# Gated recurrence and capacity routing into eight experts: a shorter routing chain ahead of the experts, with both instruction orders fitted again

## The chip, the cores and the metric

The kernel runs on one core of one Trainium2 chip. The metric is device microseconds of one execution, as a median of several runs. One core has TensorE (PE, matmul), VectorE (DVE), ScalarE (ACT), GpSimd (POOL) and SyncE (SP, which issues transfers), each with its own instruction queue, and 16 DMA engines.

## The reference

Two stages, cut to what matters. The first is a recurrence over 768 steps for 4 x 8 heads of width 48; its output becomes 3072 tokens of width 384. The second gives every token to one of 8 experts, with exactly 384 places each, by going through all token-expert scores in falling order.

```python
for t in range(S):                                  # a normalised to at most 0.999 in magnitude
    S_re, S_im = ar * S_re - ai * S_im + kv[t], ar * S_im + ai * S_re
    y[:, :, t] = einsum('bhd,bhde->bhe', q[:, :, t], S_re)
x = y.transpose(0, 2, 1, 3).reshape(N, DM)          # N = 3072, DM = 384
logits = x @ w_gate                                 # [N, 8]
for idx in argsort(-logits.flatten()):              # cap = N // 8
    tok, e = idx // 8, idx % 8
    if assigned[tok] < 0 and counts[e] < cap:
        assigned[tok] = e; counts[e] += 1
for e in range(8):
    out[assigned == e] = relu(x[assigned == e] @ w1[e]) @ w2[e]
```

## The kernel before, in words

**First half** (`attention`). The 3072 tokens go in 24 units of 128, in eight groups of three. VectorE, ScalarE and GpSimd turn the decay into running products and angles; VectorE rotates keys and queries (`f<-kq,CS`); a transfer restacks them per head; TensorE does scores (`sc`), state (`U`) and output (`y`), and last the pick matmuls (`FN`, tile `xp`), which put a unit's 128 tokens in rows beside their 8 logits. ScalarE evicts the token part (`XE`, tile `x`, stored to DRAM as `xd`), and VectorE reduces the logits (`LR`, tile `lg`). `xp` has a single buffer: the next unit's `FN` waits for this unit's `XE` and `LR`. Where TensorE would idle, filler matmuls (`hot`) are put in.

**Routing** (`Router`). Expert by expert, the kernel looks for the one that fills first. `scale` takes the extremes of all logits across partitions, `quantize` turns scores into 24-bit integers. `find` searches the cut value for all experts at once in five levels of 32 thresholds: VectorE compares all tokens with them (`ind`), TensorE counts (`cnt`), VectorE compares the counts with what is needed (`cs`, `f`), and TensorE adds the step to the thresholds (`thr`). It ends with each token's position in the chosen expert (`pi`) and the expert's weight rows (`eidx`). `slots` turns positions into the expert's list of tokens (`idx`): position = 32 x high + low, two compares give one-hot rows (`o`: 12 and 32 wide), and a count matmul of the low one-hot with the high one-hot, multiplied by the token's row and column number (`rh`), gives them. `update` removes the chosen expert from the scores and picks each token's next best: that readies the next search.

**Second half** (`experts`). GpSimd gathers weights (`w1t`, `w2t`) and tokens (`xg`) by indirect transfers. Expert 0 runs in fp32: transposes (`turn`), first layer (`hidden`), second layer (`last`). Experts 1 to 7 run as three products of split halves (`w1h`, `w1l`, `xh`, `xl`, `hh`, `hl`, `w2h`, `w2l`), the splits made by ScalarE and VectorE. 18 warm-up matmuls stand ahead of expert 0. Route e + 1 runs while expert e is computed, on the same engines.

**Order.** Every operation is first put in a list with a cost, its dependences and a priority; `in_order` plays the list against one queue per engine, and the instructions are then issued in that order, which the engines keep. In the first half the priority is the unit's number plus `OFF[kind]`; in the second it is a due time, reckoned back from the end, less `M_OFF[kind]`. With `slack`, VectorE may be given a less urgent step while an urgent one is about to become ready.

All instructions go through one helper, so the profile's line is L130 almost everywhere and rows are told apart by their tiles.

Of the kernel before, what the change touches and what calls it, by code (L numbers as in the profile page):

```python
# [8 lines left out]
F32 = mybir.dt.float32  # L9
# [3 lines left out]
I32 = mybir.dt.int32  # L13
AF = mybir.ActivationFunctionType
# [23 lines left out]
LEAD_R = 8  # L38
GRID = [2.0 ** 19, 2.0 ** 14, 2.0 ** 9, 2.0 ** 4, 1.0]

# [9 lines left out]
def constants(nc, con, z, w_gate):  # L50
# [20 lines left out]
    t("i32f", [128, 32])  # L71
    t("wd", [128, 8])
    t("cidx", [128, NT])
# [7 lines left out]
    t("lg", [128, NT, E])  # L81
# [3 lines left out]
    t("ext", [128, 2, B])  # L85
# [86 lines left out]
def in_order(ops, step, hop, wait, done_, start, slack, late=None):  # L172
# [23 lines left out]
    while len(done) < len(ops):  # L196
        pick = None
        for e, xs in ready.items():
            if xs:
                t = max(free[e], min(o.at for o in xs))  # L200
                o = min((o for o in xs if o.at <= t), key=lambda o: (o.prio, o.at, o.n))
                if slack and e == "dve":
                    h = min((o for o in xs if o.at <= t + 1.0), key=lambda o: (o.prio, o.at, o.n))
                    if h.prio < o.prio - 1500.0:
                        o = min((o for o in xs if o.at <= t and t + o.cost <= h.at + slack),
                                key=lambda o: (o.prio, o.at, o.n), default=h)
                t = max(t, o.at)
                if pick is None or t < pick[0]:
                    pick = t, o
# [25 lines left out]
def attention(nc, real, tc, z, q, k, a_re, a_im, v_tok, xd, later):  # L235
# [222 lines left out]
    def unit(i):  # L458
# [97 lines left out]
        def logits():  # L556
            v.tensor_reduce(z.lg[:, i], mine["xp"][:, :, 96:104].rearrange("p a e -> p e a"), op=OP.add, axis=AX.X)
            if i % 6 == 5:
                r = slice(i - 5, i + 1)
                lg = z.lg[:, r].rearrange("p c e -> p (c e)")  # L560
                v.tensor_reduce(z.ext[:, 0, b:b + 1], lg, op=OP.max, axis=AX.X)
                v.tensor_reduce(z.ext[:, 1, b:b + 1], lg, op=OP.min, axis=AX.X)
# [77 lines left out]
OFF = {"A1": 7.7532, "F1": -8.0, "F10": -0.2852, "F11": 6.1629, "F2": 1.0958, "F3": 3.1048, "F4": 3.0098, "F5": -8.0, "F6": 8.0, "F7": -6.5322, "F8": 3.2365, "F9": 5.0508, "FL": 2.946, "FL<": -3.9259, "FN": 4.3835, "G1": -0.6071, "G2": 4.4992, "G3": 8.0, "G4": -8.0, "G5": -5.9505, "K": 1.9006, "KC": -0.4768, "LR": -3.8173, "MK": -2.5243, "MX": -4.6482, "N0": 0.976, "N1": -8.0, "N2": -5.5169, "P0": -6.2872, "R0": -7.514, "R1": -4.516, "R2": 3.2639, "R3": 4.827, "R4": -4.8476, "R5": -0.5791, "S": 6.954, "SC": 3.4101, "SC<": -8.0, "ST": 0.3675, "ST<": -0.421, "T1": 7.9956, "T2": 6.9667, "T3": -8.0, "TL": 5.7027, "UA": -3.4084, "UA<": -5.1223, "WM": 0.1274, "XC": 7.799, "XC<": -7.3842, "XE": 4.4086, "XS": 0.7846, "la": -5.6357, "later": -8.0, "li": -5.3368, "lk": -1.3428, "lv": 6.2134, "RK": -2.7051, "RQ": -3.6666, "table": -0.5748, "CA": 3.7656, "BE": -7.9653}  # L640
# [6 lines left out]
class Router:  # L647
# [11 lines left out]
    def masks(self, nc):  # L659
# [6 lines left out]
        g.iota(z.i32f, pattern=[[1, 32]], base=0, **kw)  # L666
        g.iota(z.wd, pattern=[[-1, 8]], base=8, **kw)
        g.iota(z.cidx, pattern=[[1, NT]], base=0, **kw)
# [36 lines left out]
    def scale(self):  # L705
        nc, z, v, t, ps = self.nc, self.z, self.nc.vector, self.mine, self.ps
        mm = t("mm", [128, 2])
        low = t("low", [128, B])
        v.tensor_scalar(low, z.ext[:, 1], -1.0, None, op0=OP.mult, op1=OP.max, accum_out=mm[:, 0:1])
        v.tensor_reduce(mm[:, 1:2], z.ext[:, 0], op=OP.max, axis=AX.X)  # L710
        mp = ps.tile([2, 128], F32, name="sm")
        nc.tensor.transpose(mp, mm, z.ident)
        m2 = t("m2", [2, 1])
        v.tensor_reduce(m2, mp, op=OP.max, axis=AX.X)
        gp = ps.tile([128, 2], F32, name="sm")
        nc.tensor.matmul(gp, m2.to_broadcast([2, 128]), z.mask[:2, :2], start=True, stop=True)
        gm = t("gm", [128, 1])
        rg = t("rg", [128, 2])
        v.tensor_scalar(rg[:, 0:1], gp[:, 1:2], 1e-30, 1.0 / KMAX, op0=OP.max, op1=OP.mult)
        v.tensor_copy(gm, gp[:, 0:1])  # L720
        v.reciprocal(rg[:, 1:2], rg[:, 0:1])
        self.gm, self.rg = gm, rg[:, 1:2]
        r = slice(NT - 6, NT)
        best(nc, z, self.wk, z.lg[:, r], z.top[:, r], z.qm[:, r], z.oh[:, r])
        self.m, self.qm, self.oh = t("m0", [128, NT]), z.qm, z.oh
        self.quantize(self.m, z.top)

    def quantize(self, key, x):
        v = self.nc.vector
        ki = self.wk.tile(x.shape, I32, name="ki")  # L730
        v.tensor_scalar(ki, x, self.gm, self.rg, op0=OP.add, op1=OP.mult)
        v.tensor_copy(key, ki)

    def merge(self, out, x, n, less=None):
        v = self.nc.vector
        part = [x[32 * c:32 * c + 32, n * c:n * c + n] for c in range(4)]
        if less is None:
            v.tensor_copy(out, part[0])
# [5 lines left out]
    def keys(self):  # L744
        self.key = self.mine("key", [128, NT, E])
        self.quantize(self.key, self.z.lg)

    def find(self, parts, by_pe, more):
# [17 lines left out]
        w = NT // parts  # L766
        for it in range(len(GRID)):
            ind = t("ind", [128, NT, 32], BF)
            for c in range(0, NT, w):
                v.tensor_tensor(ind[:, c:c + w], bc(m[:, c:c + w], 32),  # L770
                                thr[:, None, 32 * it:32 * it + 32].to_broadcast([128, w, 32]), op=OP.is_ge)
            both = ps.tile([128, 128], F32, name="cnt")
            whole = both[:32, :E]
            for lot in range(0, NT, w):
                with nc.one():
                    for c in range(lot, lot + w) if by_pe else ():
                        nc.tensor.matmul(whole, ind[:, c], oh[:, c], start=(c == 0), stop=(c == NT - 1))
                    for c in range(lot, lot + w, 4) if not by_pe else ():
                        nc.tensor.matmul(both[:, :32], ind[:, c:c + 4].rearrange("p c j -> p (c j)"),
# [10 lines left out]
            else:  # L790
                v.tensor_scalar(f, cnt, 0.0, -1.0, op0=OP.is_ge, op1=OP.max, accum_out=fm)
            nc.tensor.matmul(thr[:, 32 * (it + 1):], self.weight[:, it].to_broadcast([32, 128]), fm.bitcast(BF)[:, 1:2].to_broadcast([32, end - 32 * it - 31]),
                             start=False, stop=(it == len(GRID) - 1), skip_group_check=True)
# [34 lines left out]
        up = t("up", [128, NT])  # L828
        v.tensor_tensor(up, ah, qm, op=OP.mult)
        v.tensor_tensor(home, home, up, op=OP.add)  # L830
        tie0 = t("tie0", [128, NT])
        v.scalar_tensor_tensor(tie0, m, lo, free, op0=OP.is_equal, op1=OP.mult)
        rt = t("rt", [128, 2])
        old = t("old", [128, NT])
        v.tensor_scalar(old, home, em, 0.0, op0=OP.is_equal, op1=OP.add, accum_out=rt[:, 0:1])
        tie = t("tie", [128, NT])
        v.scalar_tensor_tensor(tie, qm, em, tie0, op0=OP.is_equal, op1=OP.mult, accum_out=rt[:, 1:2])
        off = ps.tile([128, 2], F32, name="sm")
        nc.tensor.matmul(off, z.tri, rt.bitcast(BF)[:, 1::2], start=True, stop=True)
# [15 lines left out]
        pi = t("pi", [128, NT], I32)  # L855
        v.scalar_tensor_tensor(pi, pos, -1.0, rank, op0=OP.add, op1=OP.add)
# [3 lines left out]
    def rest(self):  # L860
# [22 lines left out]
        pi = t("pi", [128, NT], I32)  # L883
        v.tensor_scalar(pi, pos, -1.0, None, op0=OP.add)
        self.found = eidx, pi

    def update(self, more):
# [16 lines left out]
        v.tensor_tensor(self.key, self.key, kn[:, None].to_broadcast([128, NT, E]), op=OP.add)  # L904
        m, qm, oh = t("m", [128, NT]), t("qm", [128, NT]), t("oh", [128, NT, E], BF)
        best(nc, z, wk, self.key, m, qm, oh)
        v.scalar_tensor_tensor(need, e2, SHUT, cc, op0=OP.mult, op1=OP.subtract)
# [7 lines left out]
    def slots(self, pi, by_pe):  # L915
# [6 lines left out]
        def be(x):  # L922
            return x[:, None].to_broadcast([128, NT, x.shape[1]])

        p2 = t("p2", [128, 2, NT], I32)
        v.tensor_scalar(p2[:, 0], pi, 5, None, op0=OP.arith_shift_right)
# [482 lines left out]
```

## Time and profile before

| | |
|---|---|
| runs, us | 530.4, 530.79, 543.11; median 530.79 |
| profiled execution, us | 533.11, with a span of 531.3 from first to last instruction |
| busy over the span | TensorE 84%, VectorE 78%, ScalarE 52%, GpSimd 14% |
| mean granted TensorE clock | 0.960 of full speed |

The span is the time from the first instruction to the last in one profiled execution; the 1.8 us beside it are outside of all instructions. A matmul's busy time overlaps the next one's, since they are pipelined, so rates are read from start to start.

### The profile page before, as it was taken

The page shows a single profiled execution, that of the slowest core. Times are in us where ns is not written, and L with a number is a line of the kernel's source. Part 1 is how long each engine was busy: PE and PEld are TensorE (multiplying, and loading weights), DVE is VectorE, ACT ScalarE, POOL GpSimd, SP SyncE. Part 2 cuts the span into 40 slices and gives each one's busy share as a digit, 9 for nine tenths or more (in the row PEclk, how much of TensorE's full clock was granted, in tenths as well). Part 3 has the DMA queues.
Part 4 walks back from the last instruction along what each step waited for, and adds up shares of the span by engine and source line. Part 5 has one row for each costly group of instructions (what it writes and reads, how often), then busy time and mean ns, then how long its engine had stood idle before and what let it go on. Part 6 is the DMA issues. An engine that isn't in the chain of part 4 may idle for free.

```text
span 531.3 us, 9644 instructions
## 1 busy us (share of the span) xinstructions
PE 447.5 (84%) x3621; PEld 394.1 (74%) x3630; DVE 415.9 (78%) x1190; ACT 274.4 (52%) x426; POOL 76.0 (14%) x95
## 2 busy tenths in 40 slices
PE   0008889899889999995589899989979999999993
PEld 0007768697769888993478579878978988999993
DVE  5989879899989999735847789798988997946330
ACT  6997859696949686511012524154341544344420
POOL 3000000000000000000121213241221232440202
PEclk9999999899989999996599999999979999999997
DMA  7865879897969676621342404461250621950101
GB/s 247 248 185 153 236 209 278 214 257 210 251 194 281 176 238 178 171 77 44 121 164 107 191 31 143 170 244 64 94 223 31 231 82 39 394 207 1 46 0 44
DMA packets 48909, 86.03 MB, mean 162 GB/s; under 512 B 5344, under 2 KB 43744, under 8 KB 46816
## 3 DMA queue, kind: packets, MB, share of 16 engines
q1 hardware_dynamic: 39104, 42.56, 27.6%
q0 software_dynamic: 6304, 38.16, 21.0%
q10 hardware_dynamic: 3456, 4.72, 2.6%
q8 instruction: 28, 0.46, 0.3%
q14 instruction: 17, 0.14, 0.1%
HBM read 53.49 MB, written 9.44 MB: 118 GB/s over the span
## 4 chain that ended last, share of the span: by engine, by line
PE 49%; DVE 18%; DMA 13%; ACT 7%; issue 6%; SPq 4%; POOL 1%; another core or an unknown queue 0%; POOLq 0%; ACTq 0%; DVEq 0%
PE acc L130 30%; SPq L130 4%; PE y L130 4%; ACT s L130 4%; PE U L130 3%; DMA s<-s 3%; PE sc L130 3%; DMA ar<-in_a_re 3%; PE xp L130 3%; DVE hl L130 2%; PE cnt L130 2%; DMA V<-in_v 2%; DVE f L130 2%; DMA KQ<-f 2%; DVE p L130 1%
## 5 line engine op out<-in xcount | busy, mean ns | idle before, releaser
L130 PE MATMUL sc<-KQ 96*128 96x128 f32 x384 | 50.2, 284 | 41.3 <-DMA KQ<-f 41.3
L130 PEld LDWEIGHTS sc<-KQ 96*128 96x128 f32 x384 | 47.3, 197 | 44.6 <-DMA KQ<-f 42.1
L130 ACT ACTIVATE hh<-acc 128x384 fp32r<-128x384 f32 x56 | 27.3, 492 | 74.6 <-PE acc L130 69.2
L130 PE MATMUL acc<-w2h,hh 128*128 128x384 f32 x168 | 53.5, 351 | 0.1
L130 PE MATMUL acc<-w2l,hh 128*128 128x384 f32 x168 | 53.4, 352 | 0.1
L130 PE MATMUL acc<-w2h,hl 128*128 128x384 f32 x168 | 53.4, 353 | 0.0
L130 PE MATMUL acc<-xh,w1h 128*128 128x384 f32 x168 | 51.0, 348 | 0.5 <-DVE hl L130 0.5
L130 PE MATMUL acc<-xh,w1l 128*128 128x384 f32 x168 | 50.2, 343 | 0.0
L130 PE MATMUL acc<-xl,w1h 128*128 128x384 f32 x168 | 49.8, 341 | 0.0
L130 DVE TENSOR_TENSOR f<-kq,CS 128x768 f32<-128x768 f32 x48 | 43.5, 951 | 0.2 <-ACT CS L130 0.2
L130 DVE SCALAR_TENSOR_TENSOR hl<-acc,hh 128x384 fp32r<-128x384 f32 x56 | 30.4, 550 | 15.0 <-ACT hh L130 14.5
L130 DVE TENSOR_TENSOR ind<-m,thr 128x768 bf16<-128x768 f32 (+1 forms) x40 | 33.7, 850 | 10.3 <-PE thr L130 9.8
L130 POOL DMA_INDIRECT out<-ot,idx x24 | 25.5, 1062 | 108.6 <-ACT ot L130 98.7
L130 ACT ACTIVATE ot<-acc 128x384 f32<-128x384 f32 x24 | 11.8, 490 | 54.7 <-issue 29.4
L130 PE MATMUL y<-am,V 128*64 128x128 f32 x384 | 37.0, 281 | 1.7 <-ACT xT L130 1.2
L130 DVE TENSOR_TENSOR am<-sc,mask 128x512 f32<-128x512 f32 x48 | 32.1, 683 | 5.0 <-PE sc L130 4.9
L130 PE MATMUL xp<-pick,xT 112*128 112x104 f32 x192 | 27.7, 290 | 8.6 <-ACT xT L130 5.7
L130 PEld LDWEIGHTS xp<-pick,xT 112*128 112x128 f32 x192 | 25.0, 201 | 12.1 <-ACT xT L130 7.3
L130 PEld LDWEIGHTS acc<-xh,w1h 128*128 128x128 f32 x168 | 30.8, 188 | 2.4 <-DVE hl L130 0.9
L130 PEld LDWEIGHTS acc<-w2l,hh 128*128 128x128 f32 x168 | 31.9, 193 | 0.9 <-DVE w2l L130 0.3
L130 PEld LDWEIGHTS acc<-w2h,hh 128*128 128x128 f32 x168 | 31.6, 192 | 0.8 <-DVE hl L130 0.5
L130 PEld LDWEIGHTS acc<-w2h,hl 128*128 128x128 f32 x168 | 31.5, 193 | 0.4
(186 smaller groups left out, 1064.4 us busy)
## 6 DMA issues: line engine op xcount, KB each, us to landing
KQ<-f SPq DMA_DIRECT2D x192, 96.4 KB, 2.4
kq<-in_k SPq DMA_DIRECT2D x8, 576.0 KB, 4.8
kq<-in_q SPq DMA_DIRECT2D x8, 576.0 KB, 6.1
V<-in_v SPq DMA_DIRECT2D x8, 576.0 KB, 9.5
xd<-x ACTq DMA_DIRECT2D x24, 192.0 KB, 2.9
ar<-in_a_re SPq DMA_DIRECT2D x6, 576.0 KB, 4.8
ai<-in_a_im SPq DMA_DIRECT2D x6, 576.0 KB, 5.8
s<-s POOLq DMA_DIRECT2D x6, 576.0 KB
```

Source lines behind the costliest of these rows:

```text
L130: r = f(*a, **k)
```

## The change

1. *Logits then eviction.* The last unit's eviction waits for its logits reduce. Extremes are taken twice, over units 0 to 17 and over the last six with the first result, in place of four times; both get across partitions by two matmuls against the identity and a reduce over 128. Scores are quantized straight into integers, without a cast.
2. *Search levels.* The first search compares in three lots of 8 units in place of two of 12, with the counts of each lot behind it, and the threshold matmul of a level is split: first the 32 columns that the next level reads.
3. *Slots in 16 bits.* Positions, one-hots and token numbers are kept as pairs of 16-bit values, so that the compares and the product have all operands in 16 bits with an innermost row of 2. One token number replaces row and column number, so `rh` is 12 wide and ScalarE's part goes. The 32-wide compare is made in two halves with the count matmuls of each behind it.
4. *Next search deferred.* What belongs to the next search (`need`, `home`) has the priority kind of `update`, the first route's steps may not be held up by slack fillers, and `hidden(0)` comes ahead of `turn(1)` in the list.
5. All values of `OFF` and `M_OFF` are new (of the logits reduce `LR` from -3.8173 to 6.6491, of the eviction `XE` from 4.4086 to -2.5219), as are some costs of the planner (`M_STEP` 0.15 to 0.12, an indirect transfer's issue 1.04 to 1.26).

```diff
-        op(("XE", i), "act", 0.46, at, out, [("FN", i), ("XS", i - 2)])
+        op(("LR", i), "dve", 0.15 if i not in (MOST - 1, NT - 1) else 0.45, at, logits, [("FN", i)])
+        op(("XE", i), "act", 0.46, at, out, [("FN", i), ("XS", i - 2)] + ([("LR", i)] if i == nu - 1 else []))
-        op(("LR", i), "dve", 0.15 if i % 6 < 5 else 0.45, at, logits, [("FN", i)])
...
+        for i in range(2):
+            nc.tensor.matmul(gp[:, i], z.ext[:, i:i + 1].to_broadcast([128, 128]), z.ident, start=True, stop=True)
+        for i, o in enumerate((OP.max, OP.min)):
+            v.tensor_reduce(lim[:, i], gp[:, i], op=o, axis=AX.X)
...
-        v.tensor_scalar(ki, x, self.gm, self.rg, op0=OP.add, op1=OP.mult)
-        v.tensor_copy(key, ki)
+        self.nc.vector.tensor_scalar(key, x, self.gm, self.rg, op0=OP.subtract, op1=OP.mult)
...
+            at = 32 * (it + 1)
+            for lo, hi in ((at, at + 32), (at + 32, end + 1)) if first and at < end else ((at, end + 1),):
+                nc.tensor.matmul(thr[:, lo:hi], self.weight[:, it].to_broadcast([32, 128]), fm.bitcast(BF)[:, 1:2].to_broadcast([32, hi - lo]),
+                                 start=False, stop=(it == len(GRID) - 1), skip_group_check=True)
...
+        if first:
+            v.tensor_tensor(home, ah, qm, op=OP.mult)
+        if more:
+            v.scalar_tensor_tensor(need, e2, SHUT, cc, op0=OP.mult, op1=OP.subtract)
...
-        nc.scalar.activation(rh[:, :, 0], o12, AF.Copy, scale=z.pid)
-        o32 = t("o32", [128, NT, 32], BF)
-        v.tensor_tensor(o32, be(z.i32f), bc(p2[:, 1], 32), op=OP.is_equal)
-        v.tensor_tensor(rh[:, :, 1], o12, bc(z.cidx, 12), op=OP.mult)
+        rh = t("rh", [128, NT, 6, 2], F16)
+        v.tensor_tensor(rh, o12, z.token[:, :, None].to_broadcast([128, NT, 6, 2]), op=OP.mult)
+        o32 = t("o32", [128, 2, NT // 2, 16, 2], F16)
+        for h in range(2):
+            c0 = h * NT // 2
+            v.tensor_tensor(o32[:, h], row(32, NT // 2),
+                            hl[:, 1][:, c0:c0 + NT // 2, None].to_broadcast([128, NT // 2, 16, 2]), op=OP.is_equal)
...
+        hidden(0)
         turn(1)
-        hidden(0)
...
-PARTS = (2, 1, 1, 1, 1, 1, 1)
+PARTS = ((0, 8, 16),) + 6 * ((0,),)
```

## Rows read from the trace of the kernel before

**Rows 1.** Busy time by stretch, us: sum and count per engine, granted clock, DMA share, GB/s.
```profile
60.00:220.00 160.00, 146.51 (x1467) 125.97 (x1473) 148.23 (x273) 121.95 (x160) 3.37 (x4) 0.98 0.80 224
...
390.00:400.00 10.00, 7.34 (x30) 6.24 (x30) 7.38 (x24) 3.44 (x4) 2.85 (x3) 0.66 0.30 95
400.00:520.00 120.00, 119.69 (x754) 112.91 (x753) 83.28 (x264) 48.55 (x102) 29.10 (x28) 1.00 0.30 114
```

**Rows 2.** Instructions in order of time, last logits to first compare: start us, duration us.
```profile
241.88 0.49 ACT L130 ACTIVATE x<-xp 128x384 f32<-128x384 f32 x1 [1.45 <-PE xp L130]
...
242.40 0.19 DVE L130 TENSOR_REDUCE lg<-xp 128x8 f32<-128x32 f32 x1 [1.75 <-ACT x L130]
...
243.38 0.37 PE L130 MATMUL sm<-ident,mm 128*2 128x128 f32 x1 [0.44 <-DVE mm L130]
...
245.84 0.55 DVE L130 TENSOR_TENSOR ind<-m,thr 128x384 bf16<-128x384 f32 x1
```

**Rows 3.** The same view inside the first search.
```profile
249.91 0.23 PE L130 MATMUL thr<-fm,weight 32*128 32x97 bf16 x1 [0.25 <-DVE f L130]
250.19 1.02 DVE L130 TENSOR_TENSOR ind<-m,thr 128x384 bf16<-128x384 f32 x2 [0.25 <-PE thr L130]
...
250.79 0.95 PE L130 MATMUL cnt<-oh,ind 128*32 128x8 bf16 x24 [0.65 <-DVE ind L130]
...
254.05 0.18 PE L130 MATMUL thr<-fm,weight 32*128 32x33 bf16 x1 [0.25 <-DVE f L130]
```

**Rows 4.** The same view, end of the first search to the gather.
```profile
256.27 0.16 DVE L130 COPY ends<-thr 128x2 f32<-128x2 f32 x1 [0.17 <-PE thr L130]
...
258.83 1.05 POOL L130 DMA_INDIRECT w1t<-in_w,eidx  x1 [119.27 <-DVE need L130]
...
261.14 1.31 DVE L130 TENSOR_TENSOR o<-i32f,p 128x288 bf16<-128x288 f32 x2
...
262.75 0.94 DVE L130 TENSOR_TENSOR ind<-m,thr 128x768 bf16<-128x768 f32 x1
...
262.87 0.82 PE L130 MATMUL cnt<-rh,o 128*32 128x24 bf16 x24 [3.00 <-DVE rh L130]
...
264.38 0.66 DVE L130 SCALAR_TENSOR_TENSOR idx<-ic 32x3 int32<-32x3 f32 x4
...
265.31 0.99 POOL L130 DMA_INDIRECT xg<-xd,idx  x1 [5.42 <-DVE cs L130]
```

**Rows 5.** The same view, transposes to the first product of expert 0.
```profile
269.18 0.36 PEld L130 LDWEIGHTS acc<-ident,xg 128*128 128x128 f32 x3
...
271.10 0.49 ACT L130 ACTIVATE x<-acc 128x384 f32<-128x384 f32 x1 [8.90 <-PE thr L130]
...
271.64 1.60 PE L130 MATMUL acc<-x,w1t 128*128 128x128 f32 x12 [1.21 <-ACT x L130]
```

**Rows 6.** VectorE's groups by shape, 241 us to the end: busy us, mean ns.
```profile
L130 DVE TENSOR_TENSOR o<-i32f,p 128x768 bf16<-128x768 f32 x8 | 7.6, 947 | 0.0
...
L130 DVE TENSOR_TENSOR ind<-m,thr 128x384 bf16<-128x384 f32 x10 | 5.2, 549 | 0.9 <-PE thr L130 0.9
...
L130 DVE TENSOR_TENSOR o<-i32f,p 128x288 bf16<-128x288 f32 x8 | 3.6, 448 | 0.0
```

**Rows 7.** Instructions in order of time, TensorE alone, among the experts.
```profile
302.25 0.20 PE L130 MATMUL thr<-fm,weight 32*128 32x97 bf16 x1 [2.20 <-DVE f L130]
...
307.90 0.63 PE L130 MATMUL acc<-xh,w1h 128*128 128x384 f32 x1
308.37 0.81 PE L130 MATMUL acc<-w2t,h 128*128 128x384 f32 x2
...
393.57 0.34 PE L130 MATMUL cnt<-oh,ind 128*128 128x32 bf16 x6 [1.24 <-DVE ind L130]
```

**Rows 8.** TensorE's groups from 308.3 to 313.6 us: busy us, mean ns.
```profile
L130 PE MATMUL acc<-w2t,h 128*128 128x384 f32 x13 | 5.4, 492 | 0.0
```

**Rows 9.** What TensorE waited for: us in total, times, longest us.
```profile
PE xp L130 <- DVE lg L130: 0.8, 1, 0.8
```

More of the change, by code (lines that the diff above doesn't have):

```diff
@@ L13 @@
 I32 = mybir.dt.int32
+I16 = mybir.dt.int16
 AF = mybir.ActivationFunctionType
@@ L37, with twice @@
 SHUT = 8192.0
-LEAD_R = 8
+MID = N // 2
+MOST = NT - 6
+PAIR = 1 + (1 << 16)
 GRID = [2.0 ** 19, 2.0 ** 14, 2.0 ** 9, 2.0 ** 4, 1.0]
+def twice(x):
+    return x[:, :, None].to_broadcast([128, NT, 2])
 def bc(x, n):
@@ L204, in in_order @@
                     if h.prio < o.prio - 1500.0:
-                        o = min((o for o in xs if o.at <= t and t + o.cost <= h.at + slack),
+                        o = min((o for o in xs if o.at <= t and t + o.cost <= h.at + (0.0 if h.kind == "first" else slack)),
                                 key=lambda o: (o.prio, o.at, o.n), default=h)
@@ L737, in merge @@
         if less is None:
-            v.tensor_copy(out, part[0])
+            v.tensor_scalar(out, part[0], more, None, op0=OP.add)
         else:
@@ L933, in slots @@
-        o32 = t("o32", [128, NT, 32], BF)
-        v.tensor_tensor(o32, be(z.i32f), bc(p2[:, 1], 32), op=OP.is_equal)
-        v.tensor_tensor(rh[:, :, 1], o12, bc(z.cidx, 12), op=OP.mult)
+        rh = t("rh", [128, NT, 6, 2], F16)
+        v.tensor_tensor(rh, o12, z.token[:, :, None].to_broadcast([128, NT, 6, 2]), op=OP.mult)
+        o32 = t("o32", [128, 2, NT // 2, 16, 2], F16)
         both = ps.tile([128, 128], F32, name="cnt")
-        with nc.one():
-            for c in range(NT) if by_pe else ():
-                nc.tensor.matmul(both[:32, :24].rearrange("p (a k) -> p a k", a=2), o32[:, c], rh[:, c],
-                                 start=(c == 0), stop=(c == NT - 1))
-            for c in range(0, NT, 4) if not by_pe else ():
-                nc.tensor.matmul(both[:, :96], o32[:, c:c + 4].rearrange("p c j -> p (c j)"),
-                                 rh[:, c:c + 4].rearrange("p c a k -> p (c a k)"), start=(c == 0), stop=(c == NT - 4))
@@ L944, in slots @@
-        ic = t("ic", [32, 2, 12])
+        for h in range(2):
+            c0 = h * NT // 2
+            v.tensor_tensor(o32[:, h], row(32, NT // 2),
+                            hl[:, 1][:, c0:c0 + NT // 2, None].to_broadcast([128, NT // 2, 16, 2]), op=OP.is_equal)
+            w = 1 if by_pe else 4
+            with nc.one():
+                for c in range(0, NT // 2, w):
+                    nc.tensor.matmul(both[:32 * w, :12 * w], o32[:, h][:, c:c + w].rearrange("p c a b -> p (c a b)"),
+                                     rh[:, c0 + c:c0 + c + w].rearrange("p c a b -> p (c a b)"),
+                                     start=(c0 + c == 0), stop=(c0 + c == NT - w))
@@ L945, in slots @@
+        idx = t("idx", [128, 3], I32, bufs=8)
         if by_pe:
[L946 to L953 removed]
+            with nc.one():
+                for s in range(4):
+                    v.tensor_scalar(idx[32 * s:32 * s + 32], both[:32, s:12:4], float(MID), None, op0=OP.add)
+        else:
+            ic = t("ic", [32, 12])
+            self.merge(ic, both, 12, more=float(MID))
+            with nc.one():
+                for s in range(4):
+                    v.tensor_copy(idx[32 * s:32 * s + 32], ic[:, s::4])
@@ L1128, in call @@
                 rate, base = RATE[self.e]
+                if name == "tensor_tensor" and all(mybir.dt.size(x.dt if isinstance(x, View) else x.dtype) == 2 for x in a):
+                    rate *= 2
                 cost = n / rate + base
```

138 lines of the change are left out of this document (62 added, 76 removed).

## The prediction

> **What bounds the kernel now.** I read busy time by stretch of time first [rows 1], then the instructions in order of time through the gap between the two halves [rows 2 to 5], then VectorE's groups by operation [rows 6], and last what TensorE waits for later [rows 7 to 9]. Three regimes follow. From 60 to 220 us VectorE is busy 148.2 of 160 us and TensorE only 146.5 with fillers in it, so the first half goes at VectorE's pace; it has 11.8 us of idle in all for a better order to win. From 400 to 520 TensorE is busy 119.7 of 120 at the full clock: there only fewer matmuls would help [rows 1]. Between them lies the gap that this change is about: the last units' results leave TensorE at 241.88 and the first product of expert 0 starts at 271.64 [rows 2, 5]. In these 29.8 us almost nothing runs but one chain of small steps: scale, five search levels, slots, gather, transposes. A microsecond taken from that chain is a microsecond for expert 0, since nothing else is late there.
>
> **Scale and first quantizing.** Before, the last logits reduce waits for the eviction of the same tile (x from 241.88, lg from 242.40), and the first search compare starts at 245.84 [rows 2]: 3.96 us from the start of x, 3.44 from the start of lg. After, the reduce starts at once: 0.52 saved. What follows it is estimated from VectorE's groups: 768 elements take 0.947 and 288 take 0.448 [rows 6], so 1.04 ns an element on a fixed part of 0.15, and operations that don't depend on each other overlap by some 0.08. After: the reduce 0.19, two extremes over 50 elements 0.32, two fp32 matmuls against the identity (0.37 by [rows 2]; the second bounded by 0.1 and 0.4, I take 0.2), two reduces over 128 elements 0.48, three dependent steps of 0.2 with their hops, a quantize of 0.3 straight to integers, three hops to and from TensorE of 0.1: near 2.75, against 3.44. Sum: 0.52 + 0.69, **-1.2** (bounds -0.5, if the choice of the last six units queues between these steps, and -1.6).
>
> **Five levels.** Two levels take 254.05 - 249.91 = 4.14 us, 2.07 each: threshold matmul 0.23, two compares 1.02 together, 24 count matmuls 0.95 that overlap the second compare, then the verdict [rows 3]. In three lots the compares cost one more fixed part: from 0.95 for 768 and 0.55 for 384 elements [rows 6] a 256-element one is 0.41, and three with the usual overlap of 0.08 make 1.09, +0.07. Behind the last compare lie 8 count matmuls and not 12, 0.04 each by 0.95 / 24: -0.16. The split threshold matmul lets the next compare start after 32 columns; the 33-column one took 0.18 against 0.23 for 97 columns [rows 3]: -0.03 on average, or +0.05 if the compare still waits for both pieces. Sum 0.1 a level, **-0.5** (bounds -0.8 and +0.2).
>
> **From the search to the gather.** Before: ends at 256.27, slot compares at 261.14, gather on POOL at 265.31 [rows 4]. In the first 4.87 us VectorE also runs the next search's six 192-element steps (0.35 each by that slope, 0.27 with the overlap) and seven steps of 8 or 24 elements (the fixed part 0.15 less the overlap, near 0.08 each), 2.2 in all. After, they are deferred. Some of them sit in bubbles where the chain waits for TensorE's prefix matmul, so I take 1.5 (bounds 0.6 and 2.2). From 261.14 to 265.31 = 4.17: two compares and a product 1.7, 24 matmuls 0.82, then the count's copy waits because the next search's compare was put in front of it (262.75, 0.94), copy, four index writes 0.66, 0.27 to POOL [rows 4]. After: in 16 bits, if VectorE takes two elements a step, half the slope between 288 elements (0.448) and 768 (0.947) [rows 6] gives 0.30 for 288 and 0.35 for 384: 0.30 + 0.30 + 0.35 + 0.35 - 3 x 0.08 = 1.06; then 0.05, the second 12 matmuls 0.41, 0.10, four writes 0.66, 0.27: 2.55. That is -1.6; unpacked the same sum is 3.25, -0.9. ScalarE's product of 24 rows leaves the path; it had run beside the second compare, so I give it nothing. Sum **-3.1** (bounds -1.5 and -4.2).
>
> No row of the kernel before is a two-tensor operation with every operand in 16 bits, so the packed price is bounded by the 1x rows and by half their slope. The Trainium skill (Vector Engine (DVE) Microarchitecture Reference, 5.1 Performance modes) says that a two-source operation takes two elements a cycle when all operands are 2 bytes wide and the innermost step is one, also when a row is read again and again, but that one 2-byte element repeated 16 times as a source ran at one a cycle. That speaks for the pair layout here (innermost row of 2), and by it the sum is 2.55; a layout that merely narrowed the types would stay at 3.25. No run shown yet tests it.
>
> **Gather and first product.** POOL's queue holds the weight load (258.83, 1.05) and then the gathers. The first transposes start at 269.18, 3.87 after the gather's issue, and the first product 2.46 after that, though x waits until 271.10 [rows 4, 5]. Three transposes, an eviction of 0.49 and two hops are about 1.3. The order now puts hidden(0) ahead of the second block's transposes, which were what TensorE held in between; I take **-0.9** (bounds 0 and -1.2). The gather now comes 4.8 sooner, the weight load only by about 2 (scale and levels), so 3.7 and not 6.5 lie between them; if the load still fills the queue the gather lands up to 2.8 later than I count. I take 0, as the product needs those weights anyway. The warm-up matmuls move with the slots; if the clock were still at its lower level, expert 0's first twelve products, 1.60 now [rows 5], would take twice that: cost 0, up to +1.6.
>
> Expert 0 therefore starts 1.2 + 0.5 + 3.1 + 0.9 = **5.7 us** sooner, near 266.
>
> **What is given back.** Route 1's search had its first compare at 262.75, ahead of the indices. Now it comes after them and after the deferred steps: indices end near 260.2, plus about 1.5, so 261.7, a gain of only 1.05; its own slots give 0.7. Expert 1's data are then 1.75 sooner, expert 0's work 5.7 sooner: 3.95 apart. Before, expert 1's first product ran at 307.90 [rows 7] while thirteen second-layer matmuls of expert 0 were still to come [rows 8]; a piece of two takes 0.81 [rows 7] and one alone 0.49, so they are 0.32 apart (4.2 us), so most of the difference has work to cover it. I take **+1.1** (bounds 0 and 4).
>
> **Later routes.** Each sheds about 0.7 us of VectorE time in its slots. TensorE is held by VectorE in two places: 2.20 before the threshold matmul at 302.25, and around 393, where it waits 1.24 for a compare [rows 7]; in 390 to 400 it is busy 7.34 at a mean clock of 0.66 [rows 1], that is 2.7 of idle and up to 3.4 lost at the lower level that follows it. Together up to 8.2. Both waits end on VectorE's search steps, which 0.7 less work shortens but does not remove, and the new order moves all of them. I take **-2.4** (bounds -8.2, and +5 for one more hole with its clock drop, sized like that of 390 to 400).
>
> **The first half's order.** Extremes: six 48-element reduces fewer, two longer ones more, about equal. All 24 units keep their matmuls. 93% busy VectorE sets the pace, so a new order is worth 0, within 3 either way (a quarter of its 11.8 idle).
>
> **Sum.** -5.7 + 1.1 - 2.4 = -7.0. The profiled execution took 533.1 for a span of 531.3; the median of the runs is 530.8, 2.3 under it, and the difference applies to it as it is: **523.8 us**. About 2%, 10.6 us, is what a measurement of this kernel tells from no change, so this counts as within it.
>
> **Rivals.** (1) Expert 1 becomes the bound: route 1 gains little, the 3.95 is given back in full and no later hole closes: 530.8 - 5.7 + 4 = 529, or 531 with a worse hole. For it: VectorE, not TensorE, ends the wait at 302.25. Against: the thirteen covering matmuls. Chance 0.20. (2) The holes close as well: -5.7 and most of the 8.2, with the clock staying up: 517, down to 514 with a better first half. For it: the drop around 393 is a consequence of one wait, and one wait less removes all of it. Against: nothing in the change touches a search level of a later route. Chance 0.27. (3) Slower: the logits reduce gets late in the first half. Its due time moves from -3.8 to +6.6, and the pick matmuls of the next unit wait for it, the PSUM tile being single. Before, TensorE waited so once, 0.8 [rows 9]. If in each of 24 units the reduce sits behind one more step of 0.95, that is +22.8: 530.8 - 7 + 22.8 = 546.6. It decides once the reduce falls past the next unit's pick matmuls; units are several microseconds apart except the last three, which speaks against it. Chance 0.07. (4) The 16-bit steps run at one element a cycle, like the rows of today [rows 6]. Slots 0.7 slower in the gap, 5.0 and not 5.7 saved, and of the later holes only a third of the relief: 530.8 - 5.0 + 1.1 - 0.8 = 526.1. For it: in every slot step one operand is still one value read 6 or 16 times over, now as a pair; against: the pair itself fills the 4 bytes that one fp32 value filled. Chance 0.08. (By the rule of the Trainium skill named above this would happen only where the innermost row is one repeated element.) The forecast itself: 0.38.
>
> **Range and chances.** The forecast's own range is 520 to 528. To hold 8 in 10 it takes in (4), most of (1) and most of (2): 514 to 532. Faster by over 2% (under 520.2): 0.27 from (2) and 0.04 from the forecast's low end, 0.31. Slower by over 2% (over 541.4): 0.06 from (3). Within: 0.63.
>
> **What would show it.** In the profile after: the last logits reduce ahead of the last eviction; 2.75 from it to the first compare; levels of about 1.97; 16-bit compares of 0.30 and 0.35; the gather 4 to 5 us and expert 0's first product 5 to 6 us nearer to the end of the first half; indices before any compare of the next search. The prediction falls if the first half's end moves by more than 3 us, if a hole like that at 393 opens or vanishes, or if TensorE stands still between expert 0 and expert 1.

## The result, and the profile after

The changed kernel takes **540.26 us** in the median of 20 runs (534.65 to 556.19); the kernel before, on the same chips, 533.91 (20 runs). The ratio is 1.0106, 95% interval 1.0069 to 1.0144: about 1.1% slower, where 523.8 us and a range of 514 to 532 were predicted. Ratios here and below leave disturbed executions out; medians don't. The profiled execution took 539.48 us, span 537.7.

Busy time by stretch of the kernel after, with the columns of [rows 1]:

```profile
60.00:220.00 160.00, 147.04 (x1420) 129.09 (x1427) 139.76 (x252) 116.27 (x150) 3.52 (x3) 0.93 0.73 210
...
300.00:310.00 10.00, 5.78 (x43) 4.01 (x42) 4.93 (x22) 5.49 (x12) 3.85 (x4) 1.00 0.91 371
310.00:320.00 10.00, 9.99 (x35) 5.30 (x36) 6.38 (x15) 2.94 (x5) 0.42 (x1) 0.83 0.01 2
...
390.00:400.00 10.00, 9.81 (x64) 9.03 (x63) 9.78 (x38) 6.42 (x16) 2.77 (x3) 1.00 0.81 327
400.00:520.00 120.00, 119.01 (x751) 111.31 (x750) 87.57 (x288) 50.67 (x102) 33.63 (x30) 1.00 0.32 120
```

Against [rows 1] the first half lost most: VectorE is busy 8.5 us less in the same 160 us (139.8 for 148.2), and TensorE's mean clock fell from 0.98 to 0.93. The hole of 390 to 400 is gone; a new one stands at 300 to 310, with a lower clock behind it.

Three milestones place the 6.4 us between the two profiled executions. The last results of the first half leave TensorE at 250.99 (before 241.84): **+9.15**. From there to expert 0's first product it is 27.23 (before 29.80): **-2.57**. From the first product to TensorE's end it is 250.9 (before 251.06): **-0.2**.

The gap after, instructions in order of time: start us, duration us, engine; it answers to [rows 2 to 5].

```profile
251.02 0.19 DVE L137 TENSOR_REDUCE logits<-xp 128x8 f32<-128x32 f32 x1 [3.03 <-PE xp L137]
251.25 0.49 ACT L137 ACTIVATE x<-xp 128x384 f32<-128x384 f32 x1 [1.45 <-DVE logits L137]
...
254.29 1.08 DVE L137 TENSOR_TENSOR ind<-m,thr 128x256 bf16<-128x256 int32 x3
...
256.35 1.08 DVE L137 TENSOR_TENSOR ind<-m,thr 128x256 bf16<-128x256 int32 x3 [0.28 <-PE thr L137]
...
264.36 0.16 DVE L137 COPY ends<-thr 128x2 f32<-128x2 f32 x1 [0.17 <-PE thr L137]
...
268.04 0.57 DVE L137 TENSOR_TENSOR o<-k,hl 128x288 f16<-128x288 f16 x2
268.53 0.30 DVE L137 TENSOR_TENSOR rh<-o,token 128x288 f16<-128x288 f16 x1
...
268.75 0.35 DVE L137 TENSOR_TENSOR o<-k,hl 128x384 f16<-128x384 f16 x1
268.88 0.47 PE L137 MATMUL cnt<-rh,o 128*32 128x12 f16 x12 [1.56 <-DVE rh L137]
...
269.28 0.80 PE L137 MATMUL acc<-ident,mask 128*128 128x128 f32 x2
...
269.79 0.95 DVE L137 TENSOR_TENSOR ind<-m,thr 128x768 bf16<-128x768 f32 x1
...
270.01 0.49 PE L137 MATMUL cnt<-rh,o 128*32 128x12 f16 x12
...
271.05 0.36 DVE L137 TENSOR_TENSOR q<-q,wd 128x192 f32<-128x192 f32 x1
271.33 0.64 DVE L137 TENSOR_SCALAR idx<-cnt 32x3 int32<-32x3 f32 x4
...
272.24 0.99 POOL L137 DMA_INDIRECT xg<-xd,idx  x1 [3.69 <-DVE idx L137]
...
276.97 0.49 PE L137 MATMUL acc<-ident,xg 128*128 128x128 f32 x3
...
278.22 1.58 PE L137 MATMUL acc<-x,w1t 128*128 128x128 f32 x12 [0.36 <-ACT x L137]
```

The reader is to see two things. The 16-bit steps are as short as was forecast, 0.30 and 0.35. But the first slot compare at 268.04 and the gather's issue at 272.24 are 4.20 apart, as before (4.17): two warming matmuls (269.28) stand between the halves of the counting matmuls, and the next search's compare (269.79) and two steps on `q` (the last at 271.05) stand in front of the indices (271.33).

In the first half, the two longest pieces of the chain that ended last (start us, length us):

```profile
83.28 10.38 DMA s<-s
...
117.60 9.65 DMA s<-s
```

And three of the waits after (total us, times, longest):

```profile
ACT xT L137 <- PE y L137: 19.6, 11, 4.3
...
ACT s L137 <- DMA s<-s: 10.4, 3, 5.2
...
PE xp L137 <- ACT xT L137: 9.5, 7, 3.3
```

s<-s is an addition that the GpSimd queue does as an accumulating transfer (step F6, for six of the ten blocks). ScalarE then takes the logarithm of the sum (F7), and the eviction xT of TensorE's tokens is queued behind that. ScalarE in order of time:

```profile
90.36 0.49 ACT L137 ACTIVATE x<-xp 128x384 f32<-128x384 f32 x1 [2.86 <-PE xp L137]
93.68 1.25 ACT L137 ACTIVATE s<-s,cb 128x1152 f32<-128x1152 f32 x1 [2.83 <-DMA s<-s]
94.84 1.15 ACT L137 ACTIVATE s<-zi 128x1152 f32<-128x1152 f32 x1
95.89 0.57 ACT L137 ACTIVATE xT<-y 128x512 f32<-128x512 f32 x1
...
106.12 0.60 ACT L137 ACTIVATE xT<-y 128x512 f32<-128x512 f32 x1 [4.35 <-PE y L137]
```

And TensorE at the same time:

```profile
86.75 2.05 PE L137 MATMUL sc<-KQ 96*128 96x128 f32 x16
...
92.39 0.81 PE L137 MATMUL hot<-cold 128*128 128x512 bf16 x3 [0.16 <-issue]
96.52 1.14 PE L137 MATMUL xp<-pick,xT 112*128 112x104 f32 x8 [3.31 <-ACT xT L137]
...
98.16 3.53 PE L137 MATMUL sc<-KQ 96*128 96x128 f32 x16
```

TensorE stands 3.31 us for xT at 96.5; from 98.3 to 108.5 its granted clock is at the lower level, and sixteen products that took 2.05 us at 86.75 take 3.53. ScalarE then waits 4.35 for TensorE. The same happens after 127.3. A third drop begins at 159.7, behind shorter waits of TensorE (0.69 for xT at 155.25, 0.71 and 0.54 for KQ at 157.26 and 158.11). Before, ScalarE waited 2.7 us for these transfers in all.

### The profile page after: what moved, and what is told of

It reads as the page before. It is cut to its first block, busy times and chain, and to the rows that moved or that the text cites. A ratio compares the mean times of both kernels' runs of the same rounds, so it can differ in the third digit from the quotient of the medians.

```text
span 537.7 us, 9586 instructions
## 1 busy us (share of the span) xinstructions
PE 454.4 (84%) x3597; PEld 401.5 (75%) x3607; DVE 410.3 (76%) x1192; ACT 271.8 (51%) x418; POOL 80.1 (15%) x95
## 4 chain that ended last, share of the span: by engine, by line
PE 45%; DMA 15%; DVE 13%; issue 11%; ACT 8%; SPq 4%; POOL 2%; POOLq 0%; DVEq 0%; ACTq 0%
PE acc L137 26%; DMA s<-s 5%; PE sc L137 5%; SPq L137 4%; ACT s L137 4%; PE y L137 3%; PE U L137 3%; PE cnt L137 3%; DMA ar<-in_a_re 2%; DMA xg<-xd,idx 2%; PE kp L137 2%; DMA V<-in_v 2%; DVE hl L137 2%; DMA KQ<-f 2%; PE xp L137 2%
## 5 line engine op out<-in xcount | busy, mean ns | idle before, releaser
L137 PE MATMUL kp<-ident,KQ 96*128 96x96 f32 x160 | 22.7, 280 | 46.4 <-DMA KQ<-f 46.1
L137 PEld LDWEIGHTS kp<-ident,KQ 96*128 96x128 f32 x160 | 17.7, 160 | 51.0 <-issue 46.1
L137 PE MATMUL acc<-xh,w1l 128*128 128x384 f32 x168 | 55.8, 345 | 0.0
L137 PE MATMUL acc<-xh,w1h 128*128 128x384 f32 x168 | 55.7, 345 | 0.0
L137 PE MATMUL acc<-xl,w1h 128*128 128x384 f32 x168 | 54.9, 340 | 0.0
L137 PE MATMUL sc<-KQ 96*128 96x128 f32 x384 | 54.5, 301 | 0.0
L137 PEld LDWEIGHTS sc<-KQ 96*128 96x128 f32 x384 | 51.6, 216 | 0.2 <-issue 0.2
L137 ACT ACTIVATE ot<-acc 128x384 f32<-128x384 f32 x24 | 11.8, 491 | 57.8 <-PE acc L137 35.3
L137 PE MATMUL y<-am,V 128*64 128x128 f32 x384 | 39.7, 300 | 0.7 <-DVE am L137 0.6
L137 PEld LDWEIGHTS U<-V,kt 128*96 128x96 f32 x320 | 32.8, 182 | 3.0 <-ACT kt L137 2.0
L137 PE MATMUL U<-V,kt 128*96 128x48 f32 x320 | 34.1, 264 | 1.1 <-ACT kt L137 0.9
```

What stands on the lines that cost most here:

```text
L137: r = f(*a, **k)
```

## The experiments

Each ratio is to the kernel before on the same chip. The h kernels stop after the first half: tokens go to the output, routing and experts are left out.

**The two searched orders, exchanged (e1 to e3).** e1 puts the offsets of before into the changed kernel's first half, e2 the new offsets into the kernel before, e3 the old offsets of both halves into the changed kernel.

```
e1: -OFF = <after>          e2: -OFF = <before>       e3: e1 and
    +OFF = <before>             +OFF = <after>            -M_OFF = <after>  +M_OFF = <before>
```


> The changed kernel with the first half's priorities (OFF) of the kernel before; all else as changed. Theory A (the new first-half order alone makes the kernel slower, the routing edits gain): first half ends near 242 us as before, the median is 3 to 5 us under the kernel before (ratio 0.990 to 0.995). Theory B (the edits of code in the first half make it late, for instance the extremes over 144 scores and the eviction that waits for the reduce, and the priorities are innocent): first half ends near 251 still, ratio 1.01. Theory C (the later first half was one execution's accident): as A for the first half, but the changed kernel would then not be slower in 20 runs, which it is; C gives a ratio near 1.00 here.

> The kernel before with the first half's priorities of the changed one and nothing else. Theory A: first half ends near 251 to 252 us, some 10 later, ratio to the kernel before 1.015 to 1.02 (the gap and the experts as before). Theory B: first half ends near 242, ratio 1.00.

> The changed kernel with OFF and M_OFF of the kernel before (the planner's new costs kept): the routing edits without either fit. If the second half's fit is worth something, this is slower than the run with the old OFF alone by what it is worth; I expect 1 to 4 us slower (ratio to before 0.993 to 1.00). If the fit of M_OFF hurts like that of OFF, it is faster, ratio 0.985 to 0.99.

e1: 539.29 us, 1.0103 (1.0043 to 1.0163). e2: 544.98, 1.0184 (1.0124 to 1.0245). e3: 539.51, 1.0103 (1.0028 to 1.0179). In the profiles the first half ends at 247.9 us in e1 and 258.2 in e2 (241.84 before). So the new offsets alone cost the kernel before 1.8%; but the old ones don't mend the changed kernel, and neither theory of e1 came out as written. A likely reason is that the same offsets put the edited list of steps (logits ahead of the eviction, extremes at units 17 and 23) in another order; h5 below shows one such shift. Exchanging the offsets behind the first half changes nothing that shows.

**The first half alone (h1 to h3): before, after, and after with the old offsets.**

> The kernel before, cut after the first half: tokens go to the output, logits and their choices are still made, the searches and the experts are left out. Both theories use it as the base: its time should be near 241.8 (last pick matmul) plus the store of the last tokens, 245 to 250 us. If it spreads by only a per cent or less, the first half's time is set by its order; if it spreads by 5 us or more from execution to execution, single profiles of the first half mean little.

> The changed kernel's first half alone (its refitted offsets, its extremes at units 17 and 23, its logits ahead of the eviction), routing and experts left out. Theory A (the first half's refitted order is what made the change slower): 7 to 10 us more than the first half of before. Rival B (the first half is equal and its 9 us in the two profiles are the spread of executions): within 2 us of it.

> The changed kernel's first half with the offsets of before: what is left of the change there is the logits ahead of the eviction and the extremes at units 17 and 23, which shift the written order a little from unit 5 on. Theory A with the offsets alone as its cause: equal to the first half of before within 1.5 us. Theory A2 (the edits of the list shift the order, too): 4 to 6 us more, as its two full profiles (247.9 and 253.4 against 241.8) had it. Rival B: all three equal.

h1 249.99, h2 258.98, h3 257.03 us: **+9.0** for the change, +7.0 with the old offsets. Their ratios to the whole kernel before are 0.4625 (0.4588 to 0.4662), 0.4800 (0.4757 to 0.4843) and 0.4789 (0.4750 to 0.4827); times 534 us, their differences are +9.3 and +8.8. The 9 us in the two profiles were no accident of one execution, and they are more than the whole loss of 6.35. Differences of the halves are given below by medians and by ratios; a ratio's interval reaches some 2 us to either side.

**The six transfers done by VectorE (h4, e7, e8), at the same places of the order.**

```
-add("F6", "pool", ..., lambda: g.dma_start(out=G_("s2"), in_=G_("s1"), accum_op=OP.add), ...)
+add("F6", "pool", ..., lambda: v.tensor_tensor(G_("s2"), G_("s2"), G_("s1"), op=OP.add), ...)
```


> The changed kernel's first half in its own order, with the six additions that the GpSimd queue does as an accumulating transfer done by VectorE at the same places. If ScalarE's wait for these transfers (8 to 10 us at about 85 and again at about 118 us), with the token eviction queued behind it, is what costs the first half its time: 4 to 8 us less than the changed first half, though VectorE gets some 8 us more of work. If these waits are covered: no faster, or slower by up to 4 us from VectorE's added work.

> The whole changed kernel in its own order, the six accumulating transfers of the first half done by VectorE at the same places. If the 17 us that this takes off the first half alone reach the end: 522 to 525 us where the changed kernel has 539 to 540, ratio 0.975 to 0.985. Rival (the experts have their own limit, a kernel that starts them earlier meets a lower clock or later weights): no better than 530, ratio 0.99 or more.

> The kernel before with the same one edit. If the accumulating transfers cost both orders, and the new order only more: 5 to 10 us faster than before, ratio 0.980 to 0.990. If the order of before hides them: within 1 us or up to 4 us slower by VectorE's 8 us of added work.

h4: 242.04 us, **16.9 less** than h2 by medians, 15.0 by ratios (0.4519). Busy time by stretch of h2:

```profile
100.00:140.00 40.00, 38.63 (x302) 33.25 (x303) 29.69 (x53) 25.41 (x31) 1.23 (x1) 0.78 0.68 187
...
60.00:220.00 160.00, 149.04 (x1345) 131.20 (x1353) 133.75 (x241) 111.71 (x142) 3.91 (x3) 0.87 0.72 201
```

And of h4:

```profile
100.00:140.00 40.00, 37.40 (x373) 31.02 (x375) 39.23 (x69) 33.77 (x41) 0.00 (x0) 1.00 0.77 225
...
60.00:220.00 160.00, 150.90 (x1532) 130.85 (x1541) 153.03 (x279) 121.96 (x160) 0.00 (x0) 1.00 0.72 208
```

TensorE is busy as long in both (149.0 and 150.9 of 160), but without the transfers it finishes 1532 matmuls and not 1345, at the full clock throughout, and VectorE, with some 8 us of work more, is busy 153 us. h2's profiled execution took 262.31 us, above its median, so here is the same row of e7, to set beside that of the kernel after (147.04 busy, 1420 matmuls, clock 0.93):

```profile
60.00:220.00 160.00, 150.75 (x1553) 130.61 (x1560) 155.27 (x286) 123.04 (x163) 0.00 (x0) 1.00 0.72 211
```

A busy share that stays high beside a falling clock is no sign of a bound. The whole kernels: e7 524.99 us, 0.986 (0.9786 to 0.9935); e8 533.83, 0.9965 (0.9908 to 1.0023), where before had 536.44 on that chip. By the ratios the transfers cost the whole changed kernel 13 us (1.0106 to 0.986), and the kernel before no more than its interval leaves open.

**Which of the six (h7, h8), and the other two orders without them (h5, h6).** h7 gives the fourth and fifth to VectorE, h8 the other four; h5 is h3 and h6 is h1 with all six given to it.

```
+lambda: v.tensor_tensor(...) if gi in (4, 5) else g.dma_start(...)          # h7; h8: (1, 2, 3, 6)
```


> First half alone, changed order; only the fourth and fifth accumulating transfer (issued at about 83 and 118 us, the two that ScalarE is seen to wait for) done by VectorE, the other four left as transfers. If the waits are the cause: most of the 17 us comes back, 243 to 249 us. If the cause is the transfers' traffic or the GpSimd queue in general: about a third of it, 252 to 255 us.

> The complement: the fourth and fifth accumulating transfer left as transfers, the other four done by VectorE. If the waits at the two are the cause: 254 to 259 us, little of the 17 us. If traffic in general is: 246 to 249 us.

> First half alone, the changed list with the offsets of before, all six accumulating transfers done by VectorE. If these transfers are the common cause of both slow orders: 242 to 246 us, some 12 us under the same order with the transfers (257.0). If the shifted order is slow by itself: 252 us or more.

> First half alone, order of before, all six accumulating transfers done by VectorE: from the whole kernel with the same edit (2.6 us under before) 246 to 249 us, where 250.0 was measured with the transfers. A larger gain, below 244, would mean that the transfers cost the order of before as much as they cost the changed one.

By medians h7 251.29 (-7.7 from h2), h8 253.49 (-5.5), h6 246.08 (-3.9 from h1), h5 254.91 (-2.1 from h3); by ratios (0.4652, 0.4676, 0.4625, 0.4727) -7.9, -6.6, 0.0 and -3.3. My theory that the two waits alone are the cause falls: the other four transfers are worth nearly as much, and by the ratios the two groups make up the whole 15.0. In the order of before, a gain from taking the transfers out is not shown. Without them, the new order is the faster one: h4 is 4.0 us under h6 by medians and 5.7 by ratios. So it is the transfers in this order, not the order by itself, that cost the 9 us.

ScalarE's wait for transfers is 7.0 us in h2, 2.4 in h7, 5.0 in h8; the clock still drops in both, at 147.7 for 10 us in h7 and at 148.8 for 24 us in h8. In h8's profiled execution (256.49 us, above its median) the wait ahead of that drop is of another kind:

```profile
148.42 1.62 PE L137 MATMUL xp<-pick,xT 112*128 112x104 f32 x8 [1.88 <-DVE logits L137]
```

The logits reduce stands on VectorE behind the sixth addition, which VectorE now does (145.55) and which there waits 1.14 us for ScalarE. And h5 shows a second cause: the list edited under the old offsets is slow without any transfer, at a full clock in its profile (1.00). There a load of V is issued behind 24 transfers of KQ that it stands ahead of in h6, and TensorE waits for V (waits of h5):

```profile
PEld y L137 <- DMA V<-in_v: 3.3, 2, 2.1
...
PE y L137 <- DMA V<-in_v: 2.4, 2, 1.7
```

That names a part of its 8.8 us over h6 (5.4 by ratios); the rest isn't settled.

**The rest alone (e5).** The changed routing and experts behind exactly the order of before in the first half. The last eviction's wait for its logits goes too.

```
 e1, and   -op(("LR", i), "dve", 0.15 if i not in (MOST - 1, NT - 1) else 0.45, ...)   # ahead of XE
           +op(("LR", i), "dve", 0.15 if i % 6 < 5 else 0.45, ...)                     # behind XE, XS
```


> The changed routing and experts behind exactly the order of before in the first half (offsets, list of steps and their costs as before; only the extremes stay at units 17 and 23). First half alone cost 9 us more after the change, the whole kernel 6.3 us more, so if the two parts add up: 2 to 3 us faster than before, ratio 0.994 to 0.996. Rival (the gain behind the first half came from the later start and is gone with it, as VectorE has less to catch up): 1.00.

533.84 us against 536.44, ratio 0.9975 (0.993 to 1.002). The medians differ by the 2.6 us that was expected, the ratio by 1.3, and the interval (-3.7 to +1.1 us) doesn't tell it from none. With the medians the parts add up (+9.0 from the halves, -2.6 here, +6.35 measured); with the ratios they do so only within the intervals (+9.3 and -1.3 against +5.7).

**The experts' hole (e4, e9).** The kind of the first search's own steps is made more urgent: e4 in e1, e9 in e7.

```
-M_OFF = {..., "first": 567.624, ...}
+M_OFF = {..., "first": 8000.0, ...}
```


> The run with the old OFF, and M_OFF of the first route raised from 568 to 8000, so that its steps are more urgent than any step of the next search. Theory D (the deferral fails because the fitted priority of the next search's first compare, 1716, stands above that of the first route, 568): the compare and the two steps on q that stood between count and indices in the changed kernel go behind, indices about 0.8 us sooner after the slot compares than in the run with the old OFF, total 0 to 1 us less. Rival (the planner fills VectorE while it waits for the count matmuls whatever the priority): same steps in front of the indices, same time within 0.3%.

> The kernel of e7 with the first search's own steps made more urgent (offset of its kind 567.6 to 8000), which gave 4 us in the changed order with the old offsets. If that adds up: 517 to 521 us, ratio 0.967 to 0.975. Rival: the orders of the experts differ by the plan's chance, and this is within 2 us of e7.

e4: 535.32 us, 0.9996 (0.9949 to 1.0043), 4.0 less than e1 (5.7 by ratios). e9: **519.92 us, 0.9752** (0.9692 to 0.9813), 5.1 less than e7 (5.8 by ratios), and faster than both kernels. The start was not what changed (the first product at 263.94 in e7, 264.55 in e9), but the experts: first product to TensorE's end 251.5 in e7 and 246.0 in e9. TensorE's wait for expert 1's tokens, 4.23 us after the change, is 3.42 in e1 and 3.55 in e7; in e4 and e9 no wait for tokens in this stretch is longer than 0.6. The changed kernel, GpSimd's queue in order of time:

```profile
297.33 0.94 POOL L137 DMA_INDIRECT w2t<-in_w,eidx  x1 [20.34 <-DVE hl L137]
298.58 0.93 POOL L137 DMA_INDIRECT w1t<-in_w,eidx  x1 [0.30 <-issue]
301.38 0.95 POOL L137 DMA_INDIRECT xg<-xd,idx  x1 [1.87 <-DVE cs L137]
```

Its TensorE:

```profile
304.89 0.89 PE L137 MATMUL acc<-w2t,h 128*128 128x384 f32 x2
310.01 0.45 PE L137 MATMUL acc<-ident,xg 128*128 128x128 f32 x1 [4.23 <-DMA xg<-xd,idx]
310.25 1.49 PE L137 MATMUL acc<-w2t,h 128*128 128x384 f32 x2
```

And TensorE in e9:

```profile
292.98 2.83 PE L137 MATMUL acc<-w2t,h 128*128 128x384 f32 x8
296.06 0.20 PE L137 MATMUL thr<-fm,weight 32*128 32x97 bf16 x1 [0.26 <-DVE f L137]
296.19 0.33 PE L137 MATMUL acc<-ident,xg 128*128 128x128 f32 x1
```

Expert 1's gather is issued 2.8 us behind its weight loads and takes 8.5 us to land where expert 0's took 4.3. It is there at about 309.9, 31.7 us after the first product. In e9 it is issued 26.0 us after the first product and used 31.6 after it. When it lands there isn't recorded; with the 5.3 us that the same gather takes in e10 it would be 31.3, an estimate. So the data come hardly sooner in e9. What differs is what stands ahead of the transposes in TensorE's queue: in e9 expert 0's second-layer products, which were ready; in the changed kernel those stand behind the transposes (310.25, at the lower clock: 1.49 for two, against 0.89 at 304.89).

**The slots first (e10).** e9, with two dependencies in the plan: the warming matmuls after the last counting matmul, the next search's keys after the indices.

```
 for c in range(...): nc.tensor.matmul(both..., rh...)
+self.placed = nc.ops[-1]                      # was behind o12: what the warming matmuls wait for
...
+if self.qm is z.qm: nc.ops[-1].deps.append(self.sent)     # key after idx
```


> The kernel of e9 with two dependencies added in the plan of the first route: the warming matmuls come after the last of the counting matmuls (not between their two halves), and the next search's keys come after the slot indices. If these two are what kept the halved compares from showing in the time from the first slot compare to the gather's issue (4.20 us after the change, 4.17 before, 3.85 in e9): 2.9 to 3.2 us there, the first product some 0.8 us sooner, the whole kernel 519 to 520 us, within what can be told. If the eviction or a queue bounds this stretch: 3.8 us or more.

The same stretch as above, in order of time, of e10:

```profile
253.86 0.57 DVE L137 TENSOR_TENSOR o<-k,hl 128x288 f16<-128x288 f16 x2
...
254.70 0.79 PE L137 MATMUL cnt<-rh,o 128*32 128x12 f16 x24 [2.60 <-DVE rh L137]
...
255.52 0.65 DVE L137 TENSOR_SCALAR idx<-cnt 32x3 int32<-32x3 f32 x4 [0.44 <-PE cnt L137]
...
256.44 0.98 POOL L137 DMA_INDIRECT xg<-xd,idx  x1 [2.08 <-DVE idx L137]
...
262.17 0.55 PE L137 MATMUL acc<-ident,xg 128*128 128x128 f32 x3 [0.22 <-DMA xg<-xd,idx]
263.29 0.94 PE L137 MATMUL acc<-x,w1t 128*128 128x128 f32 x6 [0.58 <-ACT x L137]
```

Compare to gather is now **2.58 us** (2.55 was forecast for the change). But gather to first product is 6.85, where it was 5.98 after the change: half of the 1.6 is given back, as the gather now travels 3.1 us behind the weight load, which takes 8.3 to land. The transposes start 8.8 after the weight load's issue in e7 and e10 alike, however soon the gather is issued behind it (4.75 and 3.11). The whole kernel: 518.87 us, 0.9762 (0.9694 to 0.9829), the same as e9 within what can be told. One of its six executions took 1223.33 us, at a full clock; why is not known.

**The plan told of it (e11).** e9, with the additions declared to the planner as VectorE's.

```
-BY_DMA = [(gi, 0) for gi in range(1, 7)]
+BY_DMA = []
```


> The kernel of e9, but the planner is told that the six additions are VectorE's, so that it writes another order of the first half with the same offsets. If only the transfers mattered: within 2 us of e9 (519.9). If the offsets fit the written order that they were searched with and any shift of it costs, as the edited list with the old offsets did: 5 to 12 us slower than e9.

527.11 us, 0.9884 (0.9815 to 0.9953), 8.2 more than e10 on the same chip by medians and 6.5 by ratios; its first half ends at 242.38 in the profile, e10's at 236.82, both at a mean clock of 1.00 from 60 to 220 us. So a truer model with the same offsets gives a slower order here: this shift of the order costs some 5.6 us in the two profiles, without a clock drop. That the offsets fit the one order that they were searched with is the likely reason, not shown beyond this and h5.

## Why the prediction was wrong

**The step that failed** is "The first half's order": "93% busy VectorE sets the pace, so a new order is worth 0, within 3 either way (a quarter of its 11.8 idle)". It measured +9.0, and the first half's end moved by 9.15, where the prediction named 3 as the move that would sink it. VectorE's idle time bounds what a better order can win. It doesn't bound what a worse one loses: there VectorE was busy 139.8 us and not 148.2. What the bound left out is that each engine keeps the order that it was given. An instruction that waits for a transfer holds what is queued behind it on its engine (xT behind F7), TensorE's hole is followed by 7 to 20 us at the lower clock (7 to 10 in the profile after, 20 in h2), and the next engine waits for that. That the transfers are the lever in the new order is shown (h4 15 to 17 us, e7 13). In the order of before they are worth 0 to 4 us (h6; e8 0.9965), which the intervals don't tell from none. That only the two visible waits do it was refuted (h8); by what ways the other four cost 5.5 to 6.6 us is open. Rival (3), a late logits reduce, named the right side and the wrong mechanism: after the change TensorE's two longest waits between 60 and 220 us, 3.31 and 3.23, are for xT. A wait like rival (3)'s stands ahead of a drop in h8, and there the edit made it.

Of the 16.5 us between 523.8 and 540.26, 3.1 lie in the starting point: 530.8 was the median of three runs, and 20 runs give 533.91. The rest is, in the two profiled executions, 9.15 in the first half, 3.1 in the gap (-2.57 for -5.7) and 1.1 behind it (-0.2 for -1.3).

**Scale** -1.2: measured from the last results leaving TensorE to the first compare 3.30 against 4.00, **-0.70**; 3.27 from the logits where 2.75 was summed, with VectorE's choice steps for the last six units between the scale steps, the case that the bound of -0.5 was for. **Levels** -0.5: first compare to ends 10.07 against 10.43, **-0.36**; a level takes 2.03, not 1.97. Both were right in sign.

**Search to gather** -3.1: **-1.16**. The deferral was nearly right (ends to slot compare 3.68 against 4.87, -1.19 for -1.5). The 16-bit part was right in its parts and wrong in its sum: 0.30 and 0.35 are in the trace, which agrees with the rule of the Trainium skill cited in the prediction (Vector Engine (DVE) Microarchitecture Reference, 5.1 Performance modes), and rival (4) falls; but the stretch is +0.03 and not -1.6. I read the deferral of the next search out of the diff; in the profile its compare still stands ahead of the indices. e10 shows the forecast stretch (2.58 for 2.55) once the warming matmuls and the next search's steps are out of the way.

**Gather and first product** -0.9: **-0.35**. Counted from the first transpose matmul in both profiles (269.29 before, 0.11 behind its weight load in [rows 5]), transposes to first product fell from 2.35 to 1.25, as forecast (1.3); gather's issue to transposes rose from 3.98 to 4.73, of which 4.3 pass until the tokens land. The likely reason is the load in the queue ahead of it, which I named, bounded by 2.8 and took as 0: in e7 and e10 the transposes start 8.8 us after the load's issue whenever the gather comes.

**Given back and later holes** +1.1 and -2.4: together -0.2. The hole at 393 closed, and another opened at 305.8, of 4.23 us with 3.4 us of lower clock behind it: rival (1), expert 1 as the bound, in substance. The thirteen covering matmuls of [rows 8] were there, but the new order put the waiting transposes ahead of part of them. e4 and e9, where the hole is gone, price it at 4 to 6 us.

## What to carry to other kernels

Idle time of the pacing engine bounds the gain of a new order, never its loss: where a list is ordered by fitted offsets, edit it and measure the part that was not meant to change, cut off by itself. For every instruction that waits for a transfer, ask what is queued behind it on its engine and how far away TensorE is from that; six short additions by transfer cost 15 to 17 us of the first half in one order and 0 to 4 in another. A step made shorter shows only if what was waiting behind it does not move into its place: read the order of the instructions in the profile, not the intention of the diff.

## What was unexpected in the hardware

A stretch with TensorE busy 149 of 160 us held 12% fewer matmuls than one busy 151, at granted clocks of 0.87 and 1.00 (h2, h4). The first half alone spread over 246.5 to 255.6 us from execution to execution in the old order and over 255.6 to 263.2 in the new one, but only 240.9 to 245.7 in the new one without the transfers, with a clock of 0.996 or more in every execution. In the old order the spread stays without them (244.7 to 253.5, clocks 0.943 to 0.992). A gather of tokens took 8.5 us to land when issued 2.8 us behind the second of two weight loads, 5.3 when issued 6.0 us behind it (e10), and 4.3 when issued 4.75 us behind one.
